# Multiplying one expert's second weight unsplit in fp32, and queueing VectorE's half of each split behind ScalarE's

## The chip, the cores and the metric

The kernel runs on one core of one Trainium2 chip. The metric is the device time of one execution in microseconds (us); lower is better. TensorE (PE) multiplies, VectorE (DVE) and ScalarE (ACT) do elementwise work, GpSimd (POOL) does elementwise work and issues indirect DMAs, SyncE (SP) issues the plain DMAs.

## The reference

```python
scores = q @ k.T / 8, masked (4 heads: last 32 positions; 4 heads: every 32nd position), softmax
x = (softmax @ v)                           # 8 x 576 = 4608 tokens, 512 wide
logits = x @ w_gate                         # 8 experts, top 1
for e in range(8):
    tok_idx = the (at most) 80 tokens of e with the largest gate
    h = np.maximum(x[tok_idx] @ w1[e], 0.0)            # 512 -> 1024
    out[tok_idx] = gate_w[tok_idx] * (h @ w2[e])       # 1024 -> 512
all other rows of out are zero
```

Inputs and output are fp32. Each expert has two weights, w1 and w2, of 2 MB each.

## The kernel before

**Attention, then router, then experts.** The first part of the kernel is the attention of the eight batches, whose order on the engines a planner fixes; it stores the 4608 token rows to the DRAM tensor xs, through the SBUF tiles xn (three of them) and xr. The change leaves this order as it is. Then the router (lines 790 to 930) picks the tokens: a chain of small DVE operations with a few matmuls, beginning with pos (line 843). Where PE would stand still it runs matmuls that nobody reads (helper `warm`, line 344); the last two such rows, 48 and 56 matmuls, stand in PE's queue ahead of the first expert. The router's result is a list of token numbers, by which POOL gathers 80 rows for each expert from xs (`gather`, line 898).

**Experts.** The weights are cut into 64 chunks of 512 KB (4 for each weight). SP loads a chunk into a free SBUF unit (line 276). To keep precision at fp16 speed, each chunk is split into two fp16 numbers: ACT writes hi = fp16(16 w) (`split_hi`, line 288), and DVE writes lo = fp16(16 w - hi) (`split_lo`, line 292), into another unit; then the raw unit is free for a new load. 19 chunks are split ahead, and then three during each half.

A *half* is one weight of one expert. There are 16, in the order up 0, up 1, down 0, up 2, down 1, ..., up 7, down 6, down 7. An up half (`up`) makes he = relu(w1 x), 80 tokens wide, with three fp16 matmuls for each product (lines 963 to 965); ACT and DVE write he as hi (line 969) and lo (line 970). A down half (`down_mm`) multiplies w2: for each 128 x 128 piece one matmul of lo (line 982, 80 columns) and one of hi with he's hi and lo side by side (line 983, 160 columns), 32 pieces in all, accumulated in the PSUM tile yp, of which there is one. After the second and the fourth of the four output groups, `add` copies one part with ACT (line 997) and adds the other with DVE (line 998) into y. Since the third group writes the tile that the first `add` reads, PE's third group waits for that DVE operation. `xprep` transposes the gathered rows on PE (line 947) and splits them (lines 949 and 950). `finish` transposes y (line 1004) and scales it by the gate on ACT (line 1009), and `scatter` writes the 80 rows to out with an indirect DMA from POOL (line 1015).

Every engine works off its own queue in the order in which the code emits. `weave` interleaves a half's matmuls with the splits, `xprep` and `finish`.

**Output.** out must be zero elsewhere. SP stores 18 blocks of zeros of 512 KB: nine during attention, and nine after the last weight load (line 743); the last loads use units that come free when half 7 (up 4) is multiplied. The first scatter waits for the zeros, since it writes the same tensor, and each later scatter waits for the one before.

Of the kernel before, what the change touches and what calls it, by code (L numbers as in the profile page):

```python
# [9 lines left out]
F32 = mybir.dt.float32  # L10
# [179 lines left out]
def moe_attention(ctx: ExitStack, tc, ql, kl, qs, ks, vl, va, vb, wg, w1, w2, cap, out):  # L190
# [59 lines left out]
    pts4 = wpool.tile([P, 32, 4, 18], F32, name="pts4")  # L250

# [41 lines left out]

    def wsplit():
        i = nsp[0]
        if i == len(todo):
            return
        nsp[0] += 1
        spl[i] = free.pop(0)
        split_hi(i)  # L300
        split_lo(i)
        free.append(raw[i])
        if len(free) > SPARE and nld[0] < len(todo):
            late.append(wload())
# [28 lines left out]
    xn = buf("xn", [P, 2, DM], NXN)  # L333
    xr, = buf("xr", [P, 2, DM])
# [478 lines left out]
    wpool3 = wctx.enter_context(tc.tile_pool(name="wpool3", bufs=1))  # L813
    nz = [NZ]
    free += [[wpool3.tile([P, CH], F32, name=f"x{i}"), []] for i in range(NX_)]
# [104 lines left out]
    for _ in range(RSPL):  # L920
        wsplit()
        flush()
    fls = rt.tile([1, 1], F32, name="fls")
# [20 lines left out]
    def xprep(e):  # L944
# [5 lines left out]
        nc.vector.scalar_tensor_tensor(xe[:, 1], t, SC, xe[:, 0], op0=ALU.mult, op1=ALU.subtract)  # L950
# [3 lines left out]
    def up(h, e):  # L954
        xe = xes[e]
        he = hes[e] = fp.tile([P, 2, 8, SLOTS], F16, name="he")
        for f4 in range(2):
# [10 lines left out]
            sl = slice(4 * f4, 4 * f4 + 4)  # L968
            nc.scalar.activation(he[:, 0, sl], hp, AF.Relu)
            nc.vector.scalar_tensor_tensor(he[:, 1, sl], hp, 0.0, he[:, 0, sl], op0=ALU.max, op1=ALU.subtract)  # L970
            yield

    def down_mm(h, e):
        he = hes[e]
        yp = psy.tile([P, 2, 512], F32, name="yp", bufs=1)
        for f in range(4):
            n0 = 160 * (f % 2)
            ab = yp[:, f // 2, n0:n0 + 160].rearrange("p (a s) -> p a s", a=2)
# [9 lines left out]
            if f % 2 == 1:  # L988
                add(e, yp, f // 2)
            yield  # L990

    def add(e, yp, g):
        if g == 0:
            ys_[e] = fp.tile([P, 4, SLOTS], F32, name="y32")
        a = yp[:, g, 0:320].rearrange("p (f a s) -> p f a s", f=2, a=2)
        yb = fp.tile([P, 2, SLOTS], F32, name="yb")
        nc.scalar.copy(yb, a[:, :, 1])
        nc.vector.tensor_tensor(ys_[e][:, 2 * g:2 * g + 2], a[:, :, 0], yb, op=ALU.add)

    def finish(e):  # L1000
        y32 = ys_[e]
        yt = psy.tile([SLOTS, 4, P], F32, name="yt")
        for f in range(4):
            nc.tensor.transpose(yt[:, f], y32[:, f], ident)
# [21 lines left out]
    zh = [-9]  # L1026
# [4 lines left out]
    for h, (e, w) in enumerate(halves):  # L1031
        tasks = [((down_mm if w else up)(h, e), 8, 0, 1)]
        goal = max(int(RDONE + PACE * (h + 1)), need(h + 1))
# [174 lines left out]
```

## Time and profile before

| | |
|---|---|
| median of 3 runs | 280.77 us (279.32 to 280.79) |
| the profiled execution's own time | 278.53 us |
| its span | 276.7 us |
| busy: PE, DVE, ACT, POOL | 209.5, 205.4, 166.7, 123.4 us |
| mean granted TensorE clock | 0.914 of full speed |

The profiled execution is 1.83 us longer than its span. All positions in time below count from the start of the span. No engine is busy through the whole span, so busy shares do not say what the end waits for; the chain of work, the queues and the waits do.

### The profile page before, as it was taken

To read this page: it belongs to the slowest core of one execution; us is meant where nothing else is said; L and a number is where in the kernel's file an instruction comes from. 1 tells how busy PE (TensorE), PEld (TensorE's weight loads), DVE (VectorE), ACT (ScalarE), POOL (GpSimd) and SP (SyncE) were. 2 spreads that over 40 slices of the span, in tenths; PEclk is the share of its full clock that TensorE was granted. 3 is DMA by queue.
4 is the path that set the end of the run, shared out by engine and by line. 5 is a ranking of instruction groups with operands and counts; after the bars stand their busy time and mean duration, and the time that the engine had idled before them with its cause. 6 is when DMAs were issued, how large, how long until landed. Compare 5 with 4: busy or idle time off the path is not lost.

```text
span 276.7 us, 10224 instructions
## 1 busy us (share of the span) xinstructions
PE 209.5 (76%) x4396; PEld 182.4 (66%) x4401; DVE 205.4 (74%) x329; ACT 166.7 (60%) x275; POOL 123.4 (45%) x170
## 2 busy tenths in 40 slices
PE   6757697987797989599868752988649778785771
PEld 6535495866775778488848441988649768785771
DVE  5897996979959888475962778849976977976830
ACT  1021659587565868369885923549675875866821
POOL 7954856696683876508584004641100000012331
PEclk9957799999997999989997987699997997997997
DMA  6999789999999999969999799556999999911101
GB/s 198 329 388 361 289 256 402 413 410 400 352 301 408 401 365 356 336 265 327 385 319 397 282 320 356 187 196 198 388 386 408 358 382 410 406 60 50 50 28 49
DMA packets 23666, 84.20 MB, mean 304 GB/s; under 512 B 3201, under 2 KB 3329, under 8 KB 23042
## 3 DMA queue, kind: packets, MB, share of 16 engines
q1 hardware_dynamic: 22594, 80.89, 78.3%
q0 software_dynamic: 1024, 2.62, 3.3%
q8 instruction: 36, 0.59, 0.8%
q14 instruction: 12, 0.10, 0.1%
HBM read 63.31 MB, written 20.19 MB: 302 GB/s over the span
## 4 chain that ended last, share of the span: by engine, by line
PE 38%; ACT 17%; DVE 16%; DMA 15%; issue 9%; POOL 4%; POOLq 0%; SPq 0%; ACTq 0%; DVEq 0%
DMA kl<-kl 7%; PE bk L471 7%; PE bk L534 5%; PE sloc L418 4%; PE yp L983 3%; PE bk L622 3%; PE bk L344 3%; DMA xs<-xn 3%; PE sstr L493 2%; POOL ptb L353 2%; DMA w<-w 2%; DMA xs<-xr 2%; ACT x L288 2%; ACT w L288 2%; DVE w L292 2%
## 5 line engine op out<-in xcount | busy, mean ns | idle before, releaser
L353 POOL COPY ptb<-ptl 32x576 f32<-32x576 f32 (+1 forms) x50 | 39.3, 786 | 14.0 <-DVE ptl L451 5.9
L418 PE MATMUL sloc<-kl,ql 128*32 128x128 f32 x576 | 23.3, 306 | 4.9 <-DMA kl<-kl 2.7
L418 PEld LDWEIGHTS sloc<-kl,ql 128*32 128x32 f32 x576 | 17.6, 122 | 13.4 <-issue 6.7
L471 PE MATMUL bk<-ptb,vl 128*64 128x160 f32 (+2 forms) x352 | 24.3, 299 | 1.2 <-POOL ptb L353 1.2
L471 PEld LDWEIGHTS bk<-ptb,vl 128*64 128x64 f32 x352 | 23.1, 149 | 3.1 <-POOL ptb L353 1.4
L349 ACT COPY xn<-bk 128x512 f32<-128x512 f32 x32 | 17.5, 585 | 9.5 <-PE bk L622 4.8
L1015 POOL DMA_INDIRECT out<-vs,ids x2 | 1.9, 948 | 47.2 <-ACT w L288 44.7
L448 POOL TENSOR_TENSOR pl<-pl,sm 128x576 f32<-128x576 f32 x16 | 18.3, 1162 | 10.5 <-DVE sm L445 10.3
L516 POOL TENSOR_TENSOR psn<-ps,sm 128x512 f32<-128x512 f32 (+1 forms) x16 | 11.7, 755 | 19.4 <-DVE sm L513 19.4
L493 PE MATMUL sstr<-ks,qs 128*18 128x36 f32 x1024 | 15.6, 201 | 5.4 <-issue 4.3
L493 PEld LDWEIGHTS sstr<-ks,qs 128*18 128x18 f32 x1024 | 12.2, 100 | 11.0 <-issue 9.4
L534 PE MATMUL bk<-pts,vs 128*64 128x72 f32 x512 | 18.1, 227 | 1.4 <-issue 1.4
L898 POOL DMA_INDIRECT xg<-xs,idx x8 | 10.0, 1256 | 20.4 <-PE xp L947 15.4
L439 ACT ACTIVATE pl<-pl 128x512 f32<-128x512 f32 (+1 forms) x16 | 10.6, 681 | 13.0 <-DVE pl L435 12.7
L344 PE MATMUL bk<-identb 128*128 128x128 bf16 x182 | 16.0, 270 | 2.7 <-DVE identb L654 2.7
L534 PEld LDWEIGHTS bk<-pts,vs 128*64 128x64 f32 x512 | 16.8, 137 | 1.7 <-issue 1.6
L353 POOL COPY pts<-pts 32x576 f32<-32x576 f32 x23 | 17.3, 752 | 1.1
L443 DVE TENSOR_REDUCE sm<-pl 128x18 f32<-128x1152 f32 x8 | 10.8, 1349 | 9.4 <-ACT pl L439 9.3
L433 DVE TENSOR_REDUCE sm<-sloc 128x8 f32<-128x512 f32 (+1 forms) x16 | 11.5, 744 | 8.1 <-PE sloc L418 8.1
L344 PEld LDWEIGHTS <-identb 128*128 128x128 bf16 x182 | 15.4, 127 | 3.2 <-DVE identb L654 2.7
L349 ACT COPY xtl<-bk 128x384 f32<-128x384 f32 x24 | 11.4, 477 | 9.6 <-PE bk L471 9.3
L349 ACT COPY xts<-bk 128x360 f32<-128x360 f32 (+1 forms) x24 | 11.9, 510 | 8.8 <-PE bk L534 7.5
(343 smaller groups left out, 813.8 us busy)
## 6 DMA issues: line engine op xcount, KB each, us to landing
w<-w SPq DMA_DIRECT2D x23, 512.0 KB, 7.4
out<-zt SPq DMA_DIRECT2D x18, 512.0 KB, 10.1
xs<-xn SPq DMA_DIRECT2D x16, 512.0 KB, 6.7
ql<-ql SPq DMA_DIRECT2D x8, 576.0 KB, 5.8
kl<-kl SPq DMA_DIRECT2D x16, 288.0 KB, 5.8
qs<-qs SPq DMA_DIRECT2D x8, 576.0 KB, 7.5
ks<-ks SPq DMA_DIRECT2D x16, 288.0 KB, 6.2
vl<-vl SPq DMA_DIRECT2D x8, 576.0 KB, 6.8
```

What stands on the lines that cost most here:

```text
L288: nc.scalar.activation(split_of(i)[0], raw[i][0], AF.Copy, scale=SC)
L344: nc.tensor.matmul(bk[0][:, 0:P], identb, identb, start=True, stop=True)
L349: nc.scalar.copy(o, i)
L353: nc.gpsimd.tensor_copy(o, i)
L418: nc.tensor.matmul(sloc[32 * g:32 * g + 32, 128 * c:128 * c + 128], tql[h][:, hh, 32 * t:32 * t + 32], tkl[h][:, :, hh, 32 * t:32 * t + 64 ...
L433: o["mx%d" % i] = op("mx", [("DVE", 0.17 + n * 64 * 0.00105)], lambda e, sv=sv, mv=mv: nc.vector.tensor_reduce(mv, sv, op=ALU.max, axis=AX ...
L443: nc.vector.tensor_reduce(s18, pl.rearrange("p u c k -> p (u c) k"), op=ALU.add, axis=AX.X)
L448: o["nl%d" % u] = op("nl", [("POOL", 1.34)], lambda e, u=u: nc.gpsimd.tensor_tensor(pl[:, u], pl[:, u], sm[:, 9 * u:9 * u + 9].unsqueeze(2 ...
L471: nc.tensor.matmul(t[64 * u:64 * u + 64, n0:n0 + z - a], tvl[:, u, c], ptb[:, c, u, a:z], start=(c == 3 * k), stop=(c == 3 * k - 1), tile_ ...
L493: nc.tensor.matmul(so[32 * g:32 * g + 18, r8], tqs[h][:, g, rr], tks[h][:, :, g, rr], start=False, stop=r8 == 7, tile_position=(0, 32 * g))
L516: o["ns%d" % i] = op("ns", [("POOL", d)], lambda e, js=js, z0=z0, z1=z1, st_=st_: nc.gpsimd.tensor_tensor(psn[:, :, z0:z1:st_], ps[:, :, j ...
L534: nc.tensor.matmul(t[64 * x:64 * x + 64, c:c + 72], tvs[:, r], pts4[:, 2 * (r % 16) + r // 16].rearrange("p h j -> p (h j)"), start=True, ...
```

## The change

1. **One weight unsplit.** WHOLE = [(3, 1)]: the four chunks of expert 3's w2 are not split. `up` writes expert 3's he as one fp32 tile with ACT alone, scaled by 16, and `down_mm` multiplies fp32 by fp32: 32 matmuls, whose result ACT copies to y in one operation, without an add.
2. **One add for a down half.** For the other experts but the last, the two adds of 160 columns become one of 320 columns after the fourth group. Expert 7 keeps two adds, on two tiles of their own (`psh`).
3. **DVE later in the queue.** The DVE operations behind he, xe and y are emitted up to LATER = 2 steps after ACT's part (list `soon`); `split_lo` is emitted one split behind `split_hi` (list `half_done`).
4. **Units.** The attention's tiles xn and xr now live as long as the weight units and are used as four of them; before, four tiles x were taken from memory that the attention had freed. So the router's own tiles, too, lie over other old tiles than before.
5. **Pace.** 2.8 splits for a half instead of 3; 41 remain after the first 19, since four chunks are left out.

```diff
@@ -248,6 +248,8 @@
     pts4 = wpool.tile([P, 32, 4, 18], F32, name="pts4")
+    xn = [wpool.tile([P, 2, DM], F32, name=f"xn{i}") for i in range(NXN)]
+    xr = wpool.tile([P, 2, DM], F32, name="xr")
@@ -291,13 +293,22 @@
 
+    half_done = []
+
     def wsplit():
         i = nsp[0]
-        if i == len(todo):
-            return
-        nsp[0] += 1
-        spl[i] = free.pop(0)
-        split_hi(i)
+        while i < len(todo) and halves[todo[i][0]] in WHOLE:
+            i = nsp[0] = nsp[0] + 1
+        if i < len(todo):
+            nsp[0] += 1
+            spl[i] = free.pop(0)
+            split_hi(i)
+            half_done.append(i)
+        if len(half_done) > 1 or (i == len(todo) and half_done):
+            wlow()
+
+    def wlow():
+        i = half_done.pop(0)
@@ -330,8 +341,6 @@
     xts = buf("xts", [P, 4, S // 2], 2)
-    xn = buf("xn", [P, 2, DM], NXN)
-    xr, = buf("xr", [P, 2, DM])
@@ -810,9 +819,8 @@
     rt = wctx.enter_context(tc.tile_pool(name="rt", bufs=1))
-    wpool3 = wctx.enter_context(tc.tile_pool(name="wpool3", bufs=1))
     nz = [NZ]
-    free += [[wpool3.tile([P, CH], F32, name=f"x{i}"), []] for i in range(NX_)]
+    free += [[t.rearrange("p x f -> p (x f)"), []] for t in xn + [xr]]
@@ -920,6 +928,7 @@
         flush()
+    wlow()
@@ -947,13 +956,18 @@
         nc.scalar.activation(xe[:, 0], t, AF.Copy, scale=SC)
-        nc.vector.scalar_tensor_tensor(xe[:, 1], t, SC, xe[:, 0], op0=ALU.mult, op1=ALU.subtract)
+        lo = lambda: nc.vector.scalar_tensor_tensor(xe[:, 1], t, SC, xe[:, 0], op0=ALU.mult, op1=ALU.subtract)
+        if e == 0:
+            lo()
+        else:
+            soon.append([0, lo])
         if e + NX < E:
             gather(e + NX)
 
     def up(h, e):
         xe = xes[e]
-        he = hes[e] = fp.tile([P, 2, 8, SLOTS], F16, name="he")
+        whole = (e, 1) in WHOLE
+        he = hes[e] = fp.tile([P, 8, SLOTS], F32, name="he") if whole else fp.tile([P, 2, 8, SLOTS], F16, name="he")
@@ -966,16 +980,39 @@
             sl = slice(4 * f4, 4 * f4 + 4)
+            if whole:
+                nc.scalar.activation(he[:, sl], hp, AF.Relu, scale=SC)
+                yield
+                continue
             nc.scalar.activation(he[:, 0, sl], hp, AF.Relu)
-            nc.vector.scalar_tensor_tensor(he[:, 1, sl], hp, 0.0, he[:, 0, sl], op0=ALU.max, op1=ALU.subtract)
+            soon.append([0, lambda hp=hp, sl=sl: nc.vector.scalar_tensor_tensor(
+                he[:, 1, sl], hp, 0.0, he[:, 0, sl], op0=ALU.max, op1=ALU.subtract)])
             yield
 
     def down_mm(h, e):
         he = hes[e]
-        yp = psy.tile([P, 2, 512], F32, name="yp", bufs=1)
+        if (e, 1) in WHOLE:
+            yp = psy.tile([P, 2, 512], F32, name="yp", bufs=1)[:, 0, 0:320].rearrange("p (f s) -> p f s", f=4)
+            y = ys_[e] = fp.tile([P, 2, 2, SLOTS], F32, name="y32")
+            for f in range(4):
+                for c in range(8):
+                    w = raw[NCH * h + c // 2][0]
+                    i = (c % 2) * DM + P * f
+                    nc.tensor.matmul(yp[:, f], w[:, i:i + P], he[:, c], start=(c == 0), stop=(c == 7))
+                    if c == 3:
+                        yield
+                if f == 3:
+                    nc.scalar.copy(y, yp)
+                yield
+            return
+        if e < E - 1:
+            yp = psy.tile([P, 2, 512], F32, name="yp", bufs=1)
+            yp = yp[:, :, 0:320].rearrange("p g (f a s) -> p g f a s", f=2, a=2)
+            yg = [yp[:, g] for g in range(2)]
+        else:
+            yg = [psh.tile([P, 4, SLOTS], F32, name="hp").rearrange("p (f a) s -> p f a s", a=2) for g in range(2)]
         for f in range(4):
-            n0 = 160 * (f % 2)
-            ab = yp[:, f // 2, n0:n0 + 160].rearrange("p (a s) -> p a s", a=2)
+            ab = yg[f // 2][:, f % 2]
@@ -985,23 +1022,35 @@
                     yield
-            if f % 2 == 1:
-                add(e, yp, f // 2)
+            if f == 0:
+                y = ys_[e] = fp.tile([P, 2, 2, SLOTS], F32, name="y32")
+            if e == E - 1 and f % 2 == 1:
+                add(y[:, f // 2], yg[f // 2][:, :, 0], yg[f // 2][:, :, 1])
+            elif f == 3:
+                add(y, yp[:, :, :, 0], yp[:, :, :, 1])
             yield
 
-    def add(e, yp, g):
-        if g == 0:
-            ys_[e] = fp.tile([P, 4, SLOTS], F32, name="y32")
-        a = yp[:, g, 0:320].rearrange("p (f a s) -> p f a s", f=2, a=2)
-        yb = fp.tile([P, 2, SLOTS], F32, name="yb")
-        nc.scalar.copy(yb, a[:, :, 1])
-        nc.vector.tensor_tensor(ys_[e][:, 2 * g:2 * g + 2], a[:, :, 0], yb, op=ALU.add)
+    def add(y, a0, a1):
+        yb = fp.tile([P, 2, 2, SLOTS], F32, name="yb")
+        yb = yb if len(y.shape) == 4 else yb[:, 0]
+        nc.scalar.copy(yb, a1)
+        soon.append([0, lambda: nc.vector.tensor_tensor(y, a0, yb, op=ALU.add)])
+
+    soon = []
+
+    def steps(g, d):
+        for _ in g:
+            for x in soon:
+                x[0] += 1
+            while soon and soon[0][0] >= d:
+                soon.pop(0)[1]()
+            yield
 
     def finish(e):
         y32 = ys_[e]
         yt = psy.tile([SLOTS, 4, P], F32, name="yt")
         for f in range(4):
-            nc.tensor.transpose(yt[:, f], y32[:, f], ident)
+            nc.tensor.transpose(yt[:, f], y32[:, f // 2, f % 2], ident)
@@ -1023,15 +1072,18 @@
 
-    zh = [-9]
+    zh, sd = [-9], [0]
     xprep(0)
     while nsp[0] < max(need(0), RDONE):
         wsplit()
     flush()
     for h, (e, w) in enumerate(halves):
-        tasks = [((down_mm if w else up)(h, e), 8, 0, 1)]
-        goal = max(int(RDONE + PACE * (h + 1)), need(h + 1))
-        m = min(goal, len(todo)) - nsp[0]
+        while nsp[0] - len(half_done) < need(h):
+            wlow()
+        tasks = [(steps((down_mm if w else up)(h, e), 0 if h == 2 * E - 1 else LATER), 8, 0, 1)]
+        rest = [i for i in range(nsp[0], len(todo)) if halves[todo[i][0]] not in WHOLE]
+        m = min(max(int(PACE * (h + 1)) - sd[0], sum(i < need(h + 1) for i in rest)), len(rest))
+        sd[0] += m
@@ -1042,7 +1094,7 @@
         for i in range(NCH * h, NCH * h + NCH):
-            free.append(spl[i])
+            free.append(raw[i] if (e, w) in WHOLE else spl[i])
@@ -1139,10 +1191,11 @@
 RDONE = 19
-PACE = 3.0
+PACE = 2.8
 SPARE = 2
 NF = 10
-NX_ = 4
+LATER = 2
+WHOLE = [(3, 1)]
```

How the queues change is shown at three places. The words in brackets are the semaphores that an instruction waits for: DMAHW is a ring of the plain DMAs, DMASW one of the indirect DMAs.

DVE's queue at the start of the router, before:

```order
L808 MAX_INDEX msk<-msk,g_87 128x8
L809 MAX_INDEX msk<-msk 128x8
L843 TENSOR_SCALAR pos<-msk 128x16 [waits DMAHW3_49,DMAHW4_49,DMAHW2_49,DMAHW5_49,DMAHW1_49,DMAHW7_49,DMAHW0_49,Activation_49]
L845 TENSOR_SCALAR scr,rank<-call,msk 128x256 [waits PE_49]
L845 TENSOR_SCALAR scr,rank<-call,msk 128x256 x2
```

The same place now:

```order
L817 MAX_INDEX msk<-msk,g_87 128x8
L818 MAX_INDEX msk<-msk 128x8
L851 TENSOR_SCALAR pos<-msk 128x16
L853 TENSOR_SCALAR scr,rank<-call,msk 128x256 [waits PE_49]
L853 TENSOR_SCALAR scr,rank<-call,msk 128x256 x2
```

The order is the same; pos no longer waits for DMAs or ACT (MAX_INDEX is the row that the trace calls FIND_INDEX8).

SP's queue from the last load that waits for the first gather on, before (qs, w, ks and so on are units, some of them old attention tiles):

```order
L276 DMA x_2468<-w 128x1024 [waits DMAHW5_49,DMASW0_49,PE_49]
L276 DMA x_2469<-w 128x1024 [waits DMAHW6_49]
L1068 TENSOR_LOAD fli [waits DVE_49]
L1068 ISA x2
L276 DMA qs_107<-w 128x1024 [waits DMAHW7_49,DVE_49]
L276 DMA w_102<-w 128x1024 [waits DMAHW0_49,DVE_49]
L276 DMA w_95<-w 128x1024 [waits DMAHW1_49,PE_49]
L276 DMA w_97<-w 128x1024 [waits DMAHW2_49,PE_49]
```

The same place now:

```order
L278 DMA xn_119<-w 128x1024 [waits DMAHW5_49,DMASW0_49]
L278 DMA xn_120<-w 128x1024 [waits DMAHW6_49]
L278 DMA ks_109<-w 128x1024 [waits DMAHW7_49,DVE_49,Activation_49]
L278 DMA w_95<-w 128x1024 [waits DMAHW0_49,PE_49]
L278 DMA w_97<-w 128x1024 [waits DMAHW1_49,PE_49]
L278 DMA w_102<-w 128x1024 [waits DMAHW2_49,DVE_49,Activation_49]
L278 DMA pl<-w 128x1024 [waits DMAHW3_49,DVE_49]
```

The load that follows the two behind the gather waited for the DVE part of the second split after it (qs is the raw unit of that split); now it waits for that of the first split (ks), and the next two wait for half 0 on PE alone, as the third and the fourth did.

DVE's queue around half 2 (down 0), before (w, pl, kl, pts are units; y is the add, he and xe belong to the up halves around it):

```order
L292 SCALAR_TENSOR_TENSOR w_101<-ptl,w_101 128x1024
L292 SCALAR_TENSOR_TENSOR pl<-psn,pl 128x1024
L970 SCALAR_TENSOR_TENSOR he<-hp,he 128x320
L292 SCALAR_TENSOR_TENSOR w_100<-pts,w_100 128x1024
L998 TENSOR_TENSOR y_3018<-yp,yb 128x160
L292 SCALAR_TENSOR_TENSOR kl_105<-vl,kl_105 128x1024
L292 SCALAR_TENSOR_TENSOR pts<-ptb,pts 128x1024
L998 TENSOR_TENSOR y_3018<-yp,yb 128x160
L292 SCALAR_TENSOR_TENSOR kl_106<-ptb,kl_106 128x1024
L950 SCALAR_TENSOR_TENSOR xe<-xp,xe 128x320
L970 SCALAR_TENSOR_TENSOR he<-hp,he 128x320
```

The same place now:

```order
L294 SCALAR_TENSOR_TENSOR w_99<-w_102,w_99 128x1024
L294 SCALAR_TENSOR_TENSOR w_101<-pl,w_101 128x1024
L988 SCALAR_TENSOR_TENSOR he<-hp,he 128x320
L294 SCALAR_TENSOR_TENSOR qs_107<-ptl,qs_107 128x1024
L294 SCALAR_TENSOR_TENSOR w_100<-psn,w_100 128x1024
L294 SCALAR_TENSOR_TENSOR kl_105<-pts,kl_105 128x1024
L1037 TENSOR_TENSOR y_2989<-yp,yb 128x320
L294 SCALAR_TENSOR_TENSOR ptl<-vl,ptl 128x1024
L959 SCALAR_TENSOR_TENSOR xe<-xp,xe 128x320
L988 SCALAR_TENSOR_TENSOR he<-hp,he 128x320
```

The two adds with two splits between them became one add of 320 columns, which stands behind all splits of the half but one.

## Rows read from the trace of the kernel before

**Rows 1.** Chain that ended last, 264 to 277 us: start, length, what.
```profile
268.26 2.60 DMA out<-w,ids
...
272.84 0.64 POOL out L1015
```

**Rows 2.** POOL in order of time: start, length, operation, idle time before and releaser.
```profile
245.87 0.97 POOL L1015 DMA_INDIRECT out<-vs,ids  x1 [44.72 <-ACT w L288]
249.34 0.93 POOL L1015 DMA_INDIRECT out<-vs,ids  x1 [2.50 <-ACT qs L1009]
...
264.08 1.68 POOL L1015 DMA_INDIRECT out<-qs,ids  x1 [2.47 <-ACT kl L288]
268.26 0.92 POOL L1015 DMA_INDIRECT out<-w,ids  x1 [2.49 <-ACT yb L997]
272.57 0.91 POOL L1015 DMA_INDIRECT out<-w,ids  x1 [3.39 <-ACTq L1069]
```

**Rows 3.** ACT in order of time, the last operation.
```profile
271.61 0.68 ACT L1009 ACTIVATE w<-yt,gt 80x512 f32<-80x512 f32 x1 [0.86 <-PE yt L1004]
```

**Rows 4.** Stretches: busy of PE, PEld, DVE, ACT, POOL, granted clock, DMA share, GB/s.
```profile
184.00:187.00 3.00, 3.00 (x85) 3.00 (x82) 2.11 (x3) 1.69 (x3) 0.95 (x1) 1.00 0.24 68
190.00:196.00 6.00, 2.92 (x66) 2.78 (x63) 6.00 (x9) 4.72 (x7) 0.35 (x1) 1.00 0.95 313
220.00:226.00 6.00, 5.71 (x134) 5.54 (x132) 5.24 (x7) 4.01 (x6) 0.00 (x0) 1.00 0.96 352
232.00:238.00 6.00, 6.00 (x139) 5.99 (x137) 4.13 (x6) 4.88 (x9) 0.00 (x0) 0.98 1.03 418
244.00:245.00 1.00, 1.00 (x33) 1.00 (x30) 1.00 (x2) 1.00 (x3) 0.00 (x0) 1.00 0.09 20
```

**Rows 5.** DMA issues in SP's queue in order of time.
```profile
188.41 0.34 SPq L276 DMA_DIRECT2D qs<-w  x1
189.54 1.28 SPq L276 DMA_DIRECT2D w<-w  x3
...
225.40 0.38 SPq L276 DMA_DIRECT2D kl<-w  x1
225.83 8.66 SPq L743 DMA_DIRECT2D out<-zt  x9
```

**Rows 6.** DVE in order of time, first operation of the router.
```profile
166.46 0.17 DVE L843 TENSOR_SCALAR pos<-msk 128x16 f32<-128x16 f32 x1 [1.97 <-DMA xs<-xr]
```

**Rows 7.** Chain that ended last, 172 to 184 us.
```profile
174.25 4.38 PE bk L344 x48
...
182.01 0.51 PE xp L947 x4
```

**Rows 8.** Who waited for whom, 182 to 277 us: total, times, longest.
```profile
PE yp L983 <- DVE y L998: 20.7, 9, 3.6
```

**Rows 9.** DVE in order of time, 186 to 190 us.
```profile
186.21 0.49 DVE L970 SCALAR_TENSOR_TENSOR he<-hp,he 128x320 f16<-128x320 f32 x1
...
188.30 1.22 DVE L292 SCALAR_TENSOR_TENSOR ks<-w,ks 128x1024 f16<-128x1024 f32 x1
189.44 0.48 DVE L970 SCALAR_TENSOR_TENSOR he<-hp,he 128x320 f16<-128x320 f32 x1
189.84 1.21 DVE L292 SCALAR_TENSOR_TENSOR w<-pl,w 128x1024 f16<-128x1024 f32 x1
```

**Rows 10.** PE in order of time, at two places.
```profile
163.76 0.94 PE L807 MATMUL call<-wgt,bon 128*128 128x256 f32 x2 [2.32 <-DVE wgt L802]
164.50 0.31 PE L344 MATMUL bk<-identb 128*128 128x128 bf16 x1
...
184.81 0.47 PE L947 MATMUL xp<-ident,xg 80*128 80x80 f32 x4
185.11 0.20 PE L963 MATMUL hp<-xe,w 128*128 128x80 f16 x1
```

**Rows 11.** Chain that ended last, 206 to 210 us.
```profile
207.61 0.07 PE yp L983
...
207.71 0.07 PE yp L983
```

## The prediction

> **What bounds the kernel now.** I read the end first, then went back to what the end waits for. The chain of work ends in scatters on POOL, each behind the landing of the one before [rows 1]. POOL's own queue shows the whole row: the first scatter at 245.87, then one every 3.4 to 4.2 us, the seventh at 268.26, the eighth at 272.57, and the span ends at 276.7, 4.13 us after that [rows 2]. The eighth waited a little for ACT, whose last result was there at 271.61 + 0.68 = 272.29 [rows 3]. Without that wait it could have gone 3.45 us behind the seventh, at 271.7. So two things end almost together: the experts' computation at 272.3, and the chain of scatters, which would be through 0.9 us earlier whatever the computation does. That is the main point here: a faster computation alone is worth 0.9 us.
>
> The chain of scatters begins when the zeros have landed: the DMA engines move 418 GB/s at 232 to 238 us and are down to a share of 0.09 at 244 to 245 [rows 4], and the first scatter follows. (The trace puts its wait down to ACT, whose result was long there.) The nine zeros stand in SP's queue from 225.83, right behind the last weight load at 225.40; the first of these 29 loads was issued at 188.41 [rows 5]. Ahead of it, at 184 to 187 us, the DMA engines have a share of 0.24 only [rows 4]: the loads wait for units. So the end hangs on when SP begins to load again, and how evenly it goes on.
>
> The computation is late for another reason: PE's down halves waited 20.7 us, 9 times, for the add on DVE [rows 8].
>
> **The change, part by part.**
>
> *Units and router.* pos waited 1.97 us for the store of xr, since its tile lay in that memory [rows 6]; the order of the changed kernel has no such wait. The matmul call is through by about 164.6 (PE's next starts at 164.50 [rows 10]), so the first operation that reads it can go at about 164.7 instead of 166.54: 1.9 us earlier. From there to the first expert the path is DVE, PE, and PE's unread matmuls without a pause until 182.01 [rows 7], so I take -1.9 us for all that follows (bounds 0, if something else is late, and -1.97).
>
> *First load.* In SP's queue it now waits for the DVE part of the first split in half 0, which stands behind he. On the old clock he starts at 186.21; he takes 0.40 from start to start and a split 1.14 [rows 9]: 186.21 + 0.40 + 1.14 = 187.75, less 1.9 is 185.85, against 188.41: -2.55 us with the router's share in it. The next two need only PE's half 0, so they follow at once, where the old queue waited until 189.54 for its second [rows 5].
>
> *Evenness of the loads.* 29 loads and 9 zeros of 512 KB (0.524 MB) at 418 GB/s take 38 x 1.25 = 47.7 us; from 188.41 to the first scatter are 57.5. In two stretches the rate was lower, 313 GB/s at 190 to 196 and 352 at 220 to 226 [rows 4], worth 6 x (1 - 313/418) + 6 x (1 - 352/418) = 2.5 us. The last loads wait for the end of half 7 on PE (225.40), so a faster PE closes the second gap, and the three early loads much of the first. Gathers share the DMA engines and keep some of it. Bounds 0 and -2.5; I take -1.5. First scatter: 245.87 - 2.55 - 1.5 = 241.8.
>
> *Scatters.* Each costs 2.5 us of waiting plus its own length, 0.91 to 1.68 [rows 2]. The mean of six steps is (268.26 - 245.87)/6 = 3.73; short ones give 3.45. The long ones (1.68 at 264.08) lie where DVE still splits, the short last one where it is nearly done. If the computation ends early, most of the seven steps are short: I take 3.5 (bounds 3.45 and 3.73), so 24.5 us, 241.8 + 24.5 = 266.3 for the eighth. A rule bears on this: the Trainium skill, page "GPSIMD Engine Reference", section "Specifications", says that GpSimd's SBUF interfaces are shared with VectorE and that DVE operations with two SBUF inputs, as the splits are, contend. By it the steps shorten once the splits are done (7 x 3.45 = 24.2 us); by the mean row they stay (26.1). The row at 245.87 is short in spite of splits, so the trace agrees only in part.
>
> *Down halves.* One add after the fourth group means that no group of the half reads behind an add of the same half, and the next use of yp is an up half later. The 20.7 us should go (bounds 0 and -20.7). What is late next is DVE: 41 splits x 1.14 + 22 of he and xe x 0.40 + 6 adds of 320 columns + 2 of 160. An add of 320 isn't shown; he, as large, costs 0.40 and two of 160 as much as 0.64: I take 0.45. Sum 46.7 + 8.8 + 2.7 + 0.6 = 58.8 us from about 181 on, so DVE could be done at 240 and isn't the later one. The DVE operations moved back by two steps delay what waits for them: he and xe are used one or more halves later, so I cost it at nothing; without that cover it is the rival below.
>
> *The fp32 half.* Each fp32 multiply is issued as two pieces (call: x2). Not shown is the piece itself, 128 x 128 weights by 80 columns. Nearest: the transposes xp, fp32 weights of 128 columns by 80 columns, (185.11 - 184.81)/4 = 0.075; call, by 256 columns, (164.50 - 163.76)/2 = 0.37 [rows 10]. 64 pieces: 4.8 to 23.7 us, against 32 x 0.10 = 3.3 split [rows 11]. I take 0.075, as the columns are the same: +1.5 us. It removes 4 splits (4.6 us of DVE), 2 of he and an add, already out of the sum above.
>
> *Computation.* 272.3 - 1.9 - 20.7 + 1.5 = 251.2. The scatters need it by 266.3, so 15 us of this gain are hidden, and the cover is wide.
>
> **Sum.** 266.3 + 4.1 = 270.4 for the span, 6.3 us less; the profiled execution's own time 278.53 becomes 272.2. The median of the runs shown stands 2.24 us above that execution, so on its scale 280.77 - 6.3 = 274.5 us.
>
> **Rivals.**
>
> *The computation stays last* (0.14). If splits that come just in time take the place of the adds, four fifths of 20.7 come back: 272.3 - 1.9 - 4.1 + 1.5 = 267.8, 1.5 us later than the eighth scatter wants it: about 276 us. For it: DVE stays nearly full. Against: 58.8 us of DVE work in 70.
>
> *The zeros move no earlier* (0.15). If something else than pos holds the router, or units come free no sooner, only the eighth scatter's 0.9 us and shorter steps are left: 245.87 + 24.2 to 26.1, so 0.6 to 2.5 us less, about 279.3. Against: the wait of pos is gone from the queue.
>
> *The whole 20 us arrive* (0.03): about 259. Against: 38 transfers can't land so early.
>
> *Slow fp32* (0.05). At 0.37 a piece the half costs 20.4 us more, and the computation ends at 270: some 2.5 us less than now, 278. Against it is the row of xp. The Trainium skill, page "TensorE: Matmul & The Clock Gate", section "Weight-path perf modes", says that fp32 weights get no fast weight load; it would make the half slower than split, but xp's 0.075 shows no load.
>
> *Slower* (0.07). If each half opens with a wait for a DVE part that now stands behind two splits, 0.40 + 2 x 1.14 = 2.7 us, sixteen of them cost 43: the computation ends at 251.2 + 43 = 294, and the time is about 302. It decides from (272.3 - 251.2)/16 = 1.3 us for a half. For it: two splits do stand ahead of the add. Against: the readers are a half away.
>
> **Numbers.** The forecast has 0.56. Its own bounds: first scatter 245.87 - 1.9 = 244.0 with steps of 3.73 ends 2.6 us below now (278.2); first scatter 240.8 with 3.45 ends 7.7 below (273.1), and runs differ by 1.5 us. The range 271 to 279 takes in these and the first and fourth rival, about 8 in 10. A measurement of this kernel tells 0.5%, 1.4 us, from no change. Faster: 0.56 + 0.14 + 0.03 + 0.05 and half of the second rival, 0.85; same 0.08; slower 0.07.
>
> **What would show it.** Right: pos at 164.5; first load near 186; first scatter near 242, steps of 3.5; PE's waits for the add gone; the last gate scaling before 260, with scatters after it; fp32 pieces 0.075 apart. Wrong: a first scatter still near 246, scatters that wait for ACT, new PE waits for splits or he, or POOL steps of 4 us with DVE at rest.

## The result, and the profile after

The changed kernel is faster: 274.84 us median of four executions (269.0 to 276.39; a fifth took 272.05) beside 280.22 for the kernel before. The ratio, which leaves disturbed executions out, is 0.9657 [0.9549, 0.9764]; on 280.77 us that is 271.1 (268.1 to 274.1). The gain is thus larger than the 6.3 us forecast, and the time lies at the lower edge of the range of 271 to 279. Over all executions timed in this study (13 of the changed kernel, 105 of the kernel before) the mean is 271.7 against 280.9 us, 9.2 us less, good to about 1.7 (standard deviations 2.9 and 3.0).

The profiled execution took 269.0 us, with a span of 267.2. POOL's queue, as in [rows 2]:

```profile
238.32 1.47 POOL L1064 DMA_INDIRECT out<-ptb,ids  x1 [46.47 <-ACT he L987]
242.28 1.28 POOL L1064 DMA_INDIRECT out<-ptb,ids  x1 [2.50 <-DMA out<-ptb,ids]
246.03 0.91 POOL L1064 DMA_INDIRECT out<-pts,ids  x1 [2.47 <-DMA out<-ptb,ids]
...
259.57 0.91 POOL L1064 DMA_INDIRECT out<-vl,ids  x1 [2.46 <-issue]
263.05 0.91 POOL L1064 DMA_INDIRECT out<-vl,ids  x1 [2.56 <-DMA out<-vl,ids]
```

ACT's last result, as in [rows 3]:

```profile
247.35 0.68 ACT L1058 ACTIVATE vl<-yt,gt 80x512 f32<-80x512 f32 x1 [0.86 <-PE yt L1053]
```

It is there at 248.03, 15.0 us ahead of the eighth scatter; no scatter waits for it. The end is the row of scatters alone, in steps of 3.4 us where nothing else runs. PE's waits for others at 176 to 275 us, as in [rows 8] (who waited for whom, total, times, longest):

```profile
PE yt L1053 <- DVE y L1037: 2.3, 2, 1.8
PE yp L1019 <- DVE qs L294: 1.0, 1, 1.0
PE hp L1019 <- DVE qs L294: 0.8, 1, 0.8
```

The wait of 20.7 us for the add is gone, and nothing of its size came instead. SP's queue, as in [rows 5], and DVE's at two places, as in [rows 6, 9]:

```profile
182.68 0.33 SPq L278 DMA_DIRECT2D ks<-w  x1
183.11 3.37 SPq L278 DMA_DIRECT2D w<-w  x3
...
216.01 0.33 SPq L278 DMA_DIRECT2D vl<-w  x1
217.19 10.50 SPq L752 DMA_DIRECT2D out<-zt  x9
```

```profile
159.91 0.16 DVE L851 TENSOR_SCALAR pos<-msk 128x16 f32<-128x16 f32 x1
...
180.99 0.49 DVE L988 SCALAR_TENSOR_TENSOR he<-hp,he 128x320 f16<-128x320 f32 x1 [0.78 <-ACT he L987]
181.40 1.22 DVE L294 SCALAR_TENSOR_TENSOR qs<-ks,qs 128x1024 f16<-128x1024 f32 x1
```

pos waits for nothing now. Stretches, as in [rows 4] (busy of PE, PEld, DVE, ACT, POOL, granted clock, DMA share, GB/s):

```profile
184.00:190.00 6.00, 6.00 (x138) 6.00 (x136) 6.00 (x9) 5.14 (x7) 0.98 (x1) 1.00 0.95 322
220.00:226.00 6.00, 6.00 (x130) 5.99 (x127) 5.97 (x7) 5.45 (x8) 0.00 (x0) 1.00 1.03 410
236.00:238.00 2.00, 1.03 (x23) 0.86 (x21) 2.00 (x4) 2.00 (x5) 0.00 (x0) 1.00 0.11 43
...
206.00:212.00 6.00, 6.00 (x113) 5.99 (x110) 5.72 (x7) 4.15 (x8) 0.00 (x0) 1.00 1.02 405
226.00:233.00 7.00, 6.84 (x153) 6.70 (x151) 5.87 (x8) 5.94 (x9) 0.00 (x0) 1.00 1.02 411
251.00:267.00 16.00, 0.00 (x0) 0.00 (x0) 0.00 (x0) 0.00 (x0) 3.65 (x4) 0.50 0.17 50
```

At 220 to 226 the DMA engines move 410 GB/s, where [rows 4] had 352. The clock is full (1.00) in every row through the experts; it is at 0.50 at 251 to 267, where PE has nothing left to do.

**Positions from the end of attention.** The attention's last store of token rows (xr) is issued anywhere from 156 to 166 us, with the old units (156.3 to 165.5) as with the new (156.5 to 163.8). So all runs are compared from the issue of that store on. Starts in us behind that store, worked out from each trace; the last two columns are the computation (first transposes to ACT's last result) and how much of it ran at the lower of TensorE's two clock levels (granted 0.5, which is 1.2 GHz):

```
kernel (run)              xr store  transp. 1st load 1st scat. 8th scat. ACT last   end  computation lower clock
before (first profile)      161.43   20.6    27.0     84.4     111.1     110.9    115.3     90.3      10.2
before (e9)                 159.66   20.7    27.1     85.2     112.2     112.0    116.7     91.3      13.7
before (e13)                156.29   22.2    28.6     87.6     116.8     116.6    121.3     94.3      20.5
before (e17)                162.32   20.5    26.9     84.5     113.4     113.1    117.6     92.6      17.1
changed (first profile)     156.95   19.0    25.7     81.4     106.1      91.1    110.3     72.1       0
changed (e1)                159.98   19.6    26.3     81.6     106.7      91.7    110.9     72.1       0
changed (e14)               157.08   19.6    26.3     81.7     106.7      91.7    110.9     72.1       0
changed, old units (e2)     161.84   20.4    27.1     82.9     107.4      92.5    111.6     72.1       0
before, new units (e3)      158.62   17.9    24.3     82.0     110.8     110.5    115.3     92.7      17.1
before, one add (e4)        165.52   20.3    26.7     83.2     109.0      97.3    113.2     77.0       6.8
changed, all split (e5)     159.16   19.9    26.8     81.5     108.0      96.5    112.2     76.6       6.8
changed, LATER 0 (e6)       156.46   19.4    25.4     82.0     108.3      93.3    112.5     74.0       0
changed, PE delayed (e7)    159.69   20.0    26.7     82.1     108.5      96.5    112.7     76.5       0
changed, 5 zeros early (e8) 160.97   18.0    24.7     75.9     102.5      90.9    106.7     72.9       0
changed, 9 zeros early (e12)163.76   19.2    27.8     40.0      94.0      93.5     98.1     74.3       0
changed, 9 zeros early (e19)160.84   19.5    27.5     40.2      93.8      93.4     98.2     73.9       0
```

### The profile page after: what moved, and what is told of

It reads as the page before. It is cut to its first block, busy times and chain, and to the rows that moved or that the text cites. A ratio compares the mean times of both kernels' runs of the same rounds, so it can differ in the third digit from the quotient of the medians.

```text
span 267.2 us, 10185 instructions
## 1 busy us (share of the span) xinstructions
PE 208.1 (78%) x4401; PEld 180.5 (68%) x4401; DVE 196.7 (74%) x315; ACT 161.1 (60%) x264; POOL 122.2 (46%) x170
## 5 line engine op out<-in xcount | busy, mean ns | idle before, releaser
L362 POOL COPY ptb<-ptl 32x576 f32<-32x576 f32 (+1 forms) x50 | 39.9, 797 | 11.7 <-PE bk L543 3.6
L427 PEld LDWEIGHTS sloc<-kl,ql 128*32 128x32 f32 x576 | 17.0, 120 | 12.9 <-issue 5.6
L427 PE MATMUL sloc<-kl,ql 128*32 128x128 f32 x576 | 22.4, 302 | 3.7 <-DMA kl<-kl 2.4
L1064 POOL DMA_INDIRECT out<-ptb,ids x2 | 2.7, 1374 | 49.0 <-ACT he L987 46.5
L457 POOL TENSOR_TENSOR pl<-pl,sm 128x576 f32<-128x576 f32 x16 | 18.3, 1163 | 10.4 <-DVE sm L454 10.2
L480 PEld LDWEIGHTS bk<-ptb,vl 128*64 128x64 f32 x352 | 20.8, 137 | 1.3 <-issue 0.8
L480 PE MATMUL bk<-ptb,vl 128*64 128x160 f32 (+2 forms) x352 | 21.6, 279 | 0.0
L906 POOL DMA_INDIRECT xg<-xs,idx x8 | 10.9, 1358 | 18.2 <-PE xp L956 11.4
L977 PE MATMUL hp<-xe,w 128*128 128x80 f16 x104 | 15.9, 202 | 0.5 <-ACT xe L958 0.5
L631 PE MATMUL bk<-ident,xtl 128*128 128x128 f32 (+1 forms) x96 | 15.1, 307 | 1.3 <-DVE g L617 1.3
```

The source lines that it names most:

```text
L362: nc.gpsimd.tensor_copy(o, i)
L427: nc.tensor.matmul(sloc[32 * g:32 * g + 32, 128 * c:128 * c + 128], tql[h][:, hh, 32 * t:32 * t + 32], tkl[h][:, :, hh, 32 * t:32 * t + 64 ...
L457: o["nl%d" % u] = op("nl", [("POOL", 1.34)], lambda e, u=u: nc.gpsimd.tensor_tensor(pl[:, u], pl[:, u], sm[:, 9 * u:9 * u + 9].unsqueeze(2 ...
L480: nc.tensor.matmul(t[64 * u:64 * u + 64, n0:n0 + z - a], tvl[:, u, c], ptb[:, c, u, a:z], start=(c == 3 * k), stop=(c == 3 * k - 1), tile_ ...
L631: nc.tensor.transpose(t[0:n, x, c], xv[:, c, x, 128 * a:128 * a + n], ident)
L977: nc.tensor.matmul(hp[:, ff], hi[:, i:i + P], xe[:, 0, c], start=(c == 0), stop=False)
```

## Experiments

Theory at the start: behind the attention the end is the row of zeros and scatters, which begins earlier because loads do; the computation, 20 us shorter, is hidden. Rivals: the units alone make the gain; the computation alone makes it; the attention is shorter.

**The changed kernel again (e1), and with the old units (e2).** e1 has no edit. e2:

```diff
-    xn = [wpool.tile([P, 2, DM], F32, name=f"xn{i}") for i in range(NXN)]
-    xr = wpool.tile([P, 2, DM], F32, name="xr")
...
+    xn = buf("xn", [P, 2, DM], NXN)
+    xr, = buf("xr", [P, 2, DM])
...
-    free += [[t.rearrange("p x f -> p (x f)"), []] for t in xn + [xr]]
+    free += [[wpool3.tile([P, CH], F32, name=f"x{i}"), []] for i in range(4)]
```

Expected of e1: 

> The changed kernel once more. In the first profiled execution 4.5 of the 9.5 us of its span that were saved lie in the attention, whose order the change leaves as it is. Theory 1: that share is a matter of the execution (of when the lower clock was granted), so the last store of token rows, at 161.43 us in the kernel before and 156.95 in the first profile, comes elsewhere this time, between 156 and 162, and the times spread over more than 2 per cent. Theory 2: the units xn and xr at other addresses make the attention faster; then the store is at 157 again, within 0.5 us. Under both theories the first scatter comes 76 to 77 us after that store begins to move on, near 81.4 us behind it, and the last 24.7 us behind the first.

Expected of e2: 

> The changed kernel with the units of before (tiles x instead of xn and xr). Theory 1 (router): the first router operation waits for the store of xr again, 1.5 to 2 us, and everything behind it comes that much later, the end too: 1.5 to 2 us above the changed kernel at an equal end of the attention. Theory 2 (addresses of the attention's tiles): besides, the attention ends 4.5 us later, as in the kernel before. Rival 3: the wait is hidden behind the unread matmuls or the zeros, and the end does not move.

Measured: e1 270.79 us (6 executions), ratio 0.967 [0.9491, 0.985]; e2 274.4 (10), 0.9849 [0.977, 0.9929]. The store of e1 comes 3.0 us later than in the first profile, as by theory 1. In e2 pos stands 5.2 us behind the store again (2.97 in e1) and the end 0.7 to 1.3 us later. Behind the store the units are worth about 1 us here. By the times e2 is further off: its mean of 274.8 is 3.0 us above that of the changed kernel, good to 2.3; what lies ahead of the store comes up with the attention below.

**The units alone (e3).** The same edit the other way round, in the kernel before. Expected: 

> The kernel before with the units of the change alone. Theory 1: the router starts 1.5 to 2 us earlier, but down halves still wait 20 us for adds, and the computation still ends last or nearly so: 1 to 3 us less than before. Theory 2: the attention is 4.5 us shorter, too: 5 to 7 us less than before.

Measured: 281.36 us, 1.014 [0.9782, 1.0497]. The first load and the first scatter come 2.4 to 2.7 us earlier than in the first profile of before, but PE waits as long for the add, and the last scatter for ACT:

```profile
PE yp L982 <- DVE y L997: 20.9, 9, 3.6
```

```profile
265.12 0.92 POOL L1014 DMA_INDIRECT out<-w,ids  x1 [2.49 <-ACT yb L996]
269.42 0.92 POOL L1014 DMA_INDIRECT out<-w,ids  x1 [3.39 <-ACTq L1068]
```

The end stays at 115.3, as in that profile: an earlier first scatter is worth nothing while the computation ends last. But this execution has more time at the lower clock. Against e17, which has as much of it and as long a computation, the computation starts 2.6 us earlier and the end comes 2.3 us earlier. So the units may be worth some 2 us in this kernel, too; the four times do not show it.

**One add alone (e4),** in the kernel before:

```diff
-            if f % 2 == 1:
-                add(e, yp, f // 2)
...
+            if e == E - 1 and f % 2 == 1:
+                add(y[:, f // 2], yg[f // 2][:, :, 0], yg[f // 2][:, :, 1])
+            elif f == 3:
+                add(y, yp[:, :, :, 0], yp[:, :, :, 1])
```

Expected: 

> The kernel before with one add for a down half (and two tiles of its own for the last half), and nothing else. Theory 1: PE's waits for the add in the middle of a half, 20.7 us, go, the computation ends more than 10 us earlier, near 255 to 262 us, but the end follows the zeros and the scatters: 2 to 4 us less than before, by evener loads and shorter scatter steps. Rival: the computation sets the end, and the whole 10 us or more arrive. Second rival: DVE, still in the old order, makes PE wait elsewhere, and nothing is gained.

Measured: 275.97 us (10), 0.9901 [0.9812, 0.999]. The add no longer holds the groups, the computation takes 77.0 instead of 90.3 us, and the last scatter follows the row's own pace:

```profile
PE yt L1010 <- DVE y L1004: 6.2, 5, 2.5
PE hp L963 <- ACT ks L288: 1.5, 1, 1.5
```

```profile
271.08 0.92 POOL L1021 DMA_INDIRECT out<-w,ids  x1 [2.45 <-issue]
274.56 0.92 POOL L1021 DMA_INDIRECT out<-w,ids  x1 [2.56 <-DMA out<-w,ids]
```

Of 13 us the end gets 2.1, against the first profile; against the mean of the four profiles of the kernel before (117.7) it gets 4.5, of the 7.0 that the whole change brings there. It is the largest part that a run shows by itself; no run has just this part and the units.

**All weights split (e5: WHOLE empty, PACE 3.0), and DVE not later (e6: LATER 0, split_lo right behind split_hi).**

Expected of e5: 

> The changed kernel with all weights split (45 splits at a pace of 3 for a half) and the other parts kept. Theory 1: the computation ends 2 to 5 us later, as 4 splits more on DVE (4.6 us) and ACT are done, less 1.5 us of PE; the distance from the store of xr to the end stays at 110 to 111 us, within 0.7 us, since scatters set it. Rival: the unsplit weight is what brings the gain, and the distance goes back by 2 us or more.

Expected of e6: 

> The changed kernel with VectorE's operations emitted right behind ScalarE's again. Theory: the order of VectorE's part is worth part of the computation, which ends 0 to 5 us later than 91.1 to 91.7 behind the store of the last token rows, but stays ahead of the eighth scatter at 106; the first load goes earlier again by about 0.3 us against the first expert. So the end stays within 1 us of the changed kernel's 110.3 to 110.9, and the time within 0.5%. Rival: the order is what removes PE's waits, the computation ends at 104 or later, scatters wait for it, and the end comes 2 us or more later.

Measured: e5 274.15 us, 0.985 [0.9737, 0.9963], computation 76.6; e6 272.18, 0.9873 [0.9787, 0.9958], 74.0. Of the computation the unsplit weight is worth 4.5 us and the order 1.9; the ends are 1.3 to 2.2 us later than the changed kernel's, where 0.7 and 1 at most were expected; 1.4 and 1.2 us of this is one gap of POOL, which the next run explains. The times are within what runs differ.

**PE delayed (e7),** 200 unread matmuls ahead of half 14:

```diff
+        if h == 14:
+            wt = psx.tile([P, 4, SLOTS], F32, name="xp")
+            for _ in range(200):
+                nc.tensor.matmul(wt[:, 0], identb, identb[:, 0:SLOTS], start=True, stop=True)
```

Expected: 

> The changed kernel with 200 unread matmuls of 80 columns (some 7 us) on PE ahead of the half before the last. Theory 1 (zeros and scatters set the end, the computation has 15 us to spare): ACT's last result comes 5 to 7 us later behind the store of xr, and the distance from the store of xr to the end stays at 110 to 111 us, within 0.7 us. Rival (the computation sets the end): that distance grows by 5 to 7 us.

Measured: computation 4.4 us longer, 273.4 us, 0.9736 [0.9596, 0.9876] against 0.9657 and 0.967 without the delay. No scatter waits for ACT, but the end is 1.8 to 2.4 us later, where 0.7 at most was expected. Of this, 1.3 lies in one gap of POOL, 3.84 us instead of 2.5 ahead of the fourth scatter, whose rows ACT had written 29 us before. Below are POOL's queue and, for 251 to 253.4 us, the DMA queues (kind, packets, MB, share of the engines' time):

```profile
249.77 0.91 POOL L1064 DMA_INDIRECT out<-pts,ids  x1 [2.48 <-DMA out<-ptb,ids]
254.52 0.91 POOL L1064 DMA_INDIRECT out<-pts,ids  x1 [3.84 <-DMA out<-pts,ids]
```

```profile
q0 software_dynamic: 64, 0.16, 23.8%
q8 instruction: 1, 0.02, 2.5%
```

The 64 packets are the third scatter's; beside them runs one transfer of 16 KB of the kind "instruction", program code by its name, and the packets take 2.0 us from the first to the end of the last instead of 0.8. e5, e6 and e8 have one such gap each (3.86, 3.69, 3.71), e13 and e17 of the kernel before as well (4.39, 4.15), and in each of them such a transfer runs beside the packets, which take 1.8 to 2.3 us; in all other steps of the runs in the table, e12 and e19 aside, they take 0.8 to 1.1. Without this gap the end in e7 would be 0.5 to 1.1 us later; no run moves the transfer alone.

**Zeros early (e8 five, e12 and e19 all nine),** ahead of the loads that follow the gather:

```diff
     more(MORE[1])
+    for i in range(5):
+        zeros(nz[0])
+        nz[0] += 1
```

Expected of e8: 

> The changed kernel, with five of the nine last blocks of zeros issued right behind the two loads that wait for the first gather, where the DMA engines are half idle. Theory 1: the zeros have all landed 4 to 6 us earlier, first scatter and end move by as much, 104 to 107 us behind the store of xr instead of 110 to 111: a time 4 to 6 us below that of the changed kernel. Rival: the gathers of the next experts' rows share the DMA engines with these zeros and come late, PE waits, and the end moves by less than 1 us or gets later.

Measured: 269.58 us (6), 0.969 [0.9623, 0.9758]. The first scatter comes 5.5 to 5.8 us earlier behind the store, the end 3.6 to 4.2.

Expected of e12: 

> The changed kernel with all nine blocks of zeros put ahead of the weight loads that follow the gather (five of them in the run before). With five, the first scatter came 75.9 us behind the store of the last token rows instead of 81.4, and the end at 106.7 instead of 110.6; its computation ended at 90.9. Theory 1 (the end stays with the row of scatters): the first scatter goes when the first results and the zeros are there, some 3 to 6 us earlier than with five, but the last scatters then wait for the computation, which the four blocks ahead of the loads delay by up to 4 x 1.25 us: it ends at 91 to 96, and the eighth scatter's place is the later of 91 to 96 and 70 to 73 plus 25 us, so 96 to 98, the end at 100 to 103, about 264 to 267 us in time. Rival (the loads become the limit): PE waits for splits of weights that came later, the computation ends behind 102, and the time is no better than 269.6.

Expected of e19: 

> The changed kernel with all nine blocks of zeros ahead of the weight loads, again. Theory: computation 74 to 75 us long with no lower clock in it, the eighth scatter right behind ACT's last result, time 254 to 263 us, median about 259. Rival (the first run was a lucky one): median above 264.

Measured: e12 259.1 us (4), where 264 to 267 was expected, e19 260.1 (6), 0.9284 [0.9205, 0.9362]. In e19, SP's and POOL's queues and ACT's last result:

```profile
177.36 10.84 SPq L752 DMA_DIRECT2D out<-zt  x9
188.31 1.46 SPq L278 DMA_DIRECT2D ks<-w  x1
```

```profile
201.08 0.96 POOL L1067 DMA_INDIRECT out<-ptb,ids  x1 [4.59 <-ACT ptb L1061]
208.93 1.22 POOL L1067 DMA_INDIRECT out<-ptb,ids  x1 [6.90 <-ACT ptb L1061]
...
251.10 0.92 POOL L1067 DMA_INDIRECT out<-vl,ids  x1 [5.31 <-ACT yb L1039]
254.59 0.92 POOL L1067 DMA_INDIRECT out<-vl,ids  x1 [2.58 <-ACTq L1124]
```

```profile
253.59 0.68 ACT L1061 ACTIVATE vl<-yt,gt 80x512 f32<-80x512 f32 x1 [0.86 <-PE yt L1056]
```

The row of scatters is gone from the end: each goes as soon as its rows are there, and the computation, only 1.8 to 2.2 us longer, ends last. This beats both kernels, and shows where most of the computation's 18 us had gone: some 12 of them come to the end once the zeros are stored early. The kernel before was not run with early zeros; its computation ends at 110.9 or later in any case.

**The attention by itself (e10 and e15 before, e11 and e16 changed),** cut behind the attention's last operation. Expected of e10: 

> The kernel before, cut off behind the attention: router and experts are left out, so out holds only half of its zeros. It times the attention by itself. The store of the last token rows was issued at 161.43, 159.66, 161.84 and 165.52 us in the four profiles with the old units, and at 156.95, 159.98, 160.97, 159.16, 159.69 and 158.62 in the six with the new ones, means 162.1 and 159.2. Theory 1 (the attention's length differs from execution to execution, whatever the kernel): this kernel and its twin with the new units have medians within 0.8 us of each other. Theory 2 (the new units, by another placement in memory, shorten the attention): this one is about 2.9 us longer than its twin. Either way some 165 us.

Expected of e11: 

> The changed kernel, cut off behind the attention in the same way (router and experts left out). Theory 1 (length differs by execution alone): within 0.8 us of its twin. Theory 2 (the new units shorten the attention): about 2.9 us shorter than its twin, and then this is the part of the gain that the tail's 5 us do not cover.

Expected of e15: 

> The kernel before, cut off behind the attention, as in the run of 171.0 us (router and experts left out). Theory 2 (the rest of the gain lies in the attention): over both sets of executions it is 2 to 3 us longer than its twin. Theory 1: within 1 us of it.

Expected of e16: 

> The changed kernel, cut off behind the attention, as in the run of 169.73 us (router and experts left out). Theory 2: over both sets 2 to 3 us shorter than its twin. Theory 1: within 1 us of it.

Measured: 171.0 and 171.32 us against 169.73 and 170.82 (6 each). Means over twelve are 170.5 and 169.9: 0.6 us, good to 1.8. A shorter attention of 2 to 3 us is not shown, nor is one of up to 2.4 us excluded: the store of xr is issued at 161.2 us on average in the six profiles with the old units and at 159.4 in the ten with the new, and either set spreads over 7 to 9 us.

**More profiles (e9, e13, e17 before, e14 changed),** without an edit.

Expected of e9: 

> The kernel before, handed in as a kernel of its own. Theory 1 (the attention's length is a matter of the execution, by the time at the lower clock; behind the last store of xr the kernel before always takes some 115.3 us): the store begins anywhere between 156 and 166 us, the span ends 115 to 116 us behind it, the ratio is 1.00 within its interval. Theory 2 (the kernel before has a slower attention by its addresses): the store comes no earlier than 161 us. If the ratio is off 1 by more than 1 per cent, the comparison itself favours one side.

Expected of e13: 

> The kernel before, for one more profile. Theory 1 (the experts' part of the kernel before, which ends with the computation, varies more than the two profiles show): the distance from the store of the last token rows to the end is 118 us or more here or in the next one. Theory 2 (that part is steady, the rest of the gain lies in the attention): 115 to 117 again.

Expected of e14: 

> The changed kernel, for one more profile. By either theory the distance from the store of the last token rows to the end is 110 to 111.5 us, since the chain of zeros and scatters sets it; a spread above 1.5 us speaks against both.

Expected of e17: 

> The kernel before, a fourth profile. Theory (its end follows the computation, and the computation the time at the lower granted clock): from the first expert's transposes to ACT's last result it takes 90.3 us with 10.2 us at the lower clock, 91.3 with 13.7 and 94.3 with 20.5, about 0.4 us more for each us; the fourth lies on that line within 0.7 us, and its end comes 0.3 to 0.9 us ahead of or behind ACT's last result plus 4.4 us. Rival (the end varies for another reason): off the line by more than 1.5 us.

Measured: 279.71, 281.09, 270.04 and 283.82 us. Behind the store the kernel before takes 115.3, 116.7, 121.3 and 117.6 us, mean 117.7 (115 to 116 was expected of e9, 118 or more of e13 by its theory 1); the changed one 110.3, 110.9 and 110.9, mean 110.7. e17's computation is 92.6 us with 17.1 at the lower clock, where the line through the others, 0.4 us for each us at the lower clock, gives 92.9. Where the clock falls is seen in stretches of e13, in pairs of one ahead of the fall and one behind it:

```profile
188.90:192.30 3.40, 0.47 (x9) 0.34 (x7) 3.40 (x5) 2.27 (x5) 0.00 (x0) 1.00 0.92 302
192.30:195.70 3.40, 3.24 (x34) 3.24 (x34) 2.37 (x3) 0.96 (x1) 0.00 (x0) 0.51 1.01 401
...
223.10:226.50 3.40, 1.10 (x21) 0.96 (x19) 1.81 (x3) 2.24 (x5) 0.00 (x0) 1.00 1.03 396
226.50:233.30 6.80, 5.54 (x68) 5.54 (x68) 4.66 (x6) 3.05 (x4) 0.00 (x0) 0.50 1.00 369
...
247.00:250.40 3.40, 0.68 (x13) 0.54 (x11) 1.81 (x3) 2.66 (x5) 0.92 (x1) 1.00 0.16 48
250.40:257.20 6.80, 5.96 (x75) 5.96 (x75) 4.62 (x6) 2.62 (x4) 1.73 (x2) 0.50 0.09 27
```

Each time PE stands still for most of a stretch (0.47 to 1.10 us busy of 3.40) and is busy through most of the next, at half the clock. Its waits for the add are 21.1 us in this execution. The first profile of before shows the same:

```profile
205.00:208.40 3.40, 1.20 (x24) 1.20 (x24) 2.95 (x5) 2.85 (x4) 0.00 (x0) 1.00 1.03 374
208.40:211.80 3.40, 3.40 (x50) 3.40 (x47) 2.32 (x3) 1.25 (x2) 0.00 (x0) 0.50 1.02 407
```

What PE waits for is the add, as in e13 at the second of the three falls shown:

```profile
227.76 0.29 PE L983 MATMUL yp<-he,x 128*128 128x160 f16 x1 [3.56 <-DVE y L998]
```

In the four profiles of the kernel before, PE waits for the add 16 times for 3.1 to 3.6 us, and the clock falls 13 times during the computation, each time at most 1.5 us before or after the end of such a wait; behind the 12 waits of 1.8 to 1.9 us it does not fall. In the changed kernel PE's longest wait during the computation is 1.8 us.

## Why the prediction was right in kind and wrong in size

**Right.** The wait of pos is gone; PE's waits for the add are gone; the computation takes 72.1 us, where the sum made it 71.1 (251.2 less 180.1); it ends 15 us ahead of the eighth scatter and is hidden there; the end is the row of scatters, in steps of 3.5 to 3.6 (forecast 3.5); loads run evenly at 220 to 226. e4 and e7 show that some microseconds of computation more or less move the end little, e12 and e19 that the zeros were the bound. The rivals in which the computation or slow fp32 stays last, or the zeros move no earlier, did not come.

**The step that failed** is the last one of the sum: "The median of the runs shown stands 2.24 us above that execution, so on its scale 280.77 - 6.3 = 274.5 us." It took the gain read in one execution for the gain in every other, and carried the 2.24 us over to the changed kernel. The four profiles show that the experts' part of the kernel before is not one number: 115.3 to 121.3 us behind the store, and the first profile is the shortest, 2.4 us below their mean. It goes with the time that the computation spends at the lower clock, 10.2 to 20.5 us, which comes behind PE's waits. The changed kernel has none of it, and ends at 110.3 to 110.9. So the change also removes a cost for which the sum had no term. The clock is not all that differs between the four: their row of scatters takes 26.7, 27.1, 29.2 and 28.9 us, and without the wait for ACT the eighth scatter would go only 0.9 us earlier in each. From mean to mean the change saves 7.0 us behind the store, and the attention's 0.6 makes 7.6 of the 9.2; where the other 1.6 comes from stays open, and it is within what these counts can tell. That the clock falls because of the waits is inferred: kernels with 20 us of waits have 10 to 20 us at the lower clock, e4 and e5 with 6.2 and 4.6 us of waits for y 6.8, the others, with 3.8 or less, none; no run changed the clock and nothing else. The Trainium skill, page "TensorE: Matmul & The Clock Gate", section "HAM oscillation — how this bites in real kernels", tells of waits for DMAs that make the clock fall, so that the work after each starts slow again. These rows agree, with waits for VectorE: 1.00 ahead, 0.50 to 0.51 behind.

**Sizes.** Against the first profile alone the forecast was too large, not too small: -6.3, where the distance to the end falls by 4.4 to 5.0. That the two misses partly cancel is luck.
- *First load*, forecast 2.55 us earlier, came 0.7 to 1.3 earlier. The step "186.21 + 0.40 + 1.14" holds for what follows he (180.99 to 182.68, 1.69), but he itself starts 5.0 us behind the first transposes instead of 4.2: it waits 0.78 for ACT's part, which stands behind a hi split now. And of the router's 2.07 us at pos only 1.0 to 1.6 arrive at the transposes; the operation behind pos now waits 0.43 us for PE's result.
- *Evenness*, -1.5: first load to first scatter took 57.5 and takes 55.2 to 55.6, so -1.8 to -2.2.
- *fp32*, +1.5: forecast 0.075 us for a piece. PE in order of time:

```profile
211.81 1.06 PE L1001 MATMUL yp<-he,xn 128*128 128x80 f32 x8
212.71 0.61 PE L1001 MATMUL yp<-he,ks 128*128 128x80 f32 x4
```

Eight pieces take 0.90 us, 0.112 each; 64 take 7.2, 3.9 more than split. The row of xp [rows 10] did not carry over from 80 x 128 weights to 128 x 128. It costs nothing, since the unsplit weight still shortens the computation by 4.5 us (e5).
- *What a measurement can tell.* The prediction put it at 0.5%. The kernel before, run against itself, gave 1.011 [1.0056, 1.0165] (e13) and 1.0192 [1.0119, 1.0265] (e17), so ratios of single sets are good to 1 to 2% here. Measured gain and forecast differ by about that much.

## What to carry to other kernels

Read the gain from several executions, counted from a common point ahead of the change, and look at how much of the affected stage runs at the lower clock: here TensorE's waits for the add cost their length and, behind most of the long ones, work at half the clock. Where a freed stage ends early and the end does not follow, look at what is queued last; here it was zeros that could have been stored 40 us sooner, and moving them in the changed kernel brought 12.3 us more (means of 271.7 and 259.4), where the change itself had brought 9.2.

## What the hardware showed beyond that

A scatter or gather takes POOL 0.91 to 0.96 us when DVE runs no split meanwhile (102 of them in the 16 profiles), and 1.2 to 1.97 in most cases when it does (110 of 154; e3's 252.30: 1.97). In the changed kernel's first profile the last split ends at 242.8 us, and every scatter from 246 us on takes 0.91. Seven steps take 24.7 to 25.2 us there and in e1 and e14, where the prediction had 24.2 with short steps throughout and 26.1 by the mean row. That fits the rule of the Trainium skill that the prediction weighed ("GPSIMD Engine Reference", "Specifications": SBUF interfaces shared with VectorE).
